# Start-up of a fused attention and MLP kernel: tile 1 on SyncE's queue in 512 B packets, ones multiplied until data come, masks of tile 2 behind MLP units, attention three units ahead

## The chip, the cores and the metric

One core of a Trainium2 chip. The metric is the device time of one execution in microseconds (us), as the median over executions; the kernel before stood at 238.68 us (238.62 to 239.02 in three executions). Profiles cover one execution and count from its first instruction, so their spans (236.7 us before) are some 2 us shorter than the times. A DMA is issued by an engine and *lands* when its data have arrived; the *tail* is the time from the last matmul's end to the end of the execution.

## The reference

Attention with 4 batches, 8 heads, 768 positions and 64 channels per head, three heads of the kind "retrieval" (causal), five "streaming" (the first four keys and a window of 64), followed by an MLP without bias on the 3072 rows of 512:

```python
stream_keep = causal & (is_sink | in_win)
mask = np.where(retr, full_mask, stream_mask)
scores = np.where(mask, scale * (q @ k.T), -1e9)
a = softmax(scores)
x = (a @ v).transpose(0, 2, 1, 3).reshape(B * S, H * D)     # 3072 x 512
h = x @ w_in                                                # 512 x 2048
return (h - np.tanh(h)) @ w_out                             # 2048 x 512
```

## The kernel before

The work is cut into 12 tiles of 256 rows. An attention unit is one tile and one pair of heads; an MLP unit is 256 columns of `h` for one tile (8 to a tile, about 2.1 us of TensorE with the output matmuls that go with it). Attention of a tile runs among the MLP units of the tile ahead of it. The Python code does not emit instructions directly. It records operations with estimated durations, simulates the engines, the two rings of DMA and their packets, and then emits the operations in the order in which the simulation started them. Each engine executes its own part of that list in order.

```python
class Plan:
    def op(self, eng, ns, fn, r=(), w=(), dma=None, prio=None, port=False, after=None, behind=None):
        ...                                   # dependencies by key; kept in self.ops
    def run(self):
        ...                                   # event simulation: who starts when
        for i in order:
            self.ops[i][2]()                  # emit
```

The loads. `paired` decides whether two neighbouring rows of q or k travel as one packet of 512 B (rows 2p and 2p+1 to partition p) or one by one in 256 B. `load` goes through SyncE in float32 and needs a cast afterwards; `load_cast` goes through GpSimd's ring and casts on the way.

```python
        def paired(nm, t):
            return nm != "v" and t == 0
        ...
        cast_qk(0, (("ACT", "ACT"), ("ACT", "DVE")), (0,))
        load_cast(1, [("rv", 0, "v", 0, 1)], "qk")        # tile 1: GpSimd's ring, 256 B
        if first:
            load_w_in(*W_IN[0], ())                       # first quarter of w_in, GpSimd's ring
            load_cast(1, (), "v")
        for n in (0, 1):
            masks(thr, "thr", range(2 * n, 2 * n + 2), added=True)
            st_T(n, "ACT", "DVE")                         # transposes of q and k on TensorE
            for f in scores(n):
                f()
        ...
        if first:
            load_w_in(*W_IN[1], ())
            load_w_in(*W_IN[2], ())
            ...
```

The plan:

```python
        AHEAD = 2.0
        for t in range(3, NTT):
            ...
            ahead = (AHEAD if t > NG else 0.0, AHEAD) if ranked(t) else (0.0, 0.0)
            SPAN[t] = (lo + cut[t % NG] - ahead[0], lo + cut[t % NG + 1] - ahead[1])
        ...
                if t == 1 and hp == HP - 1:
                    fs.append(lambda: masks(thr, "thr", range(H)))
```

The softmax here doesn't subtract the row's maximum and nothing guards it: scores larger than these inputs give would overflow.

## Time and profile before

| | before |
|---|---|
| median time | 238.68 us |
| span of the profile | 236.7 us |
| first matmul, last matmul's end | 6.0, 231.8 us |
| clock records of TensorE begin at full share | 14.95 us |
| first MLP unit | 18.93 us |
| w_in in four pieces, landed | 17.05, 23.67, 26.36, 28.98 us |
| q and k of tile 1 landed | 11.4 to 13.5 us |
| first MLP unit of tile 2, of tile 3 | 58.83, 78.75 us |

The table is read as a start-up: until 18.9 us TensorE has no MLP work. From then on the MLP is the bulk of it. The lines of the profile from which these follow are shown in the prediction.

### The profile page before, as it was taken

What the parts mean: (1) busy time and instruction counts of PE and PEld (TensorE: products, weight loads), DVE (VectorE), ACT (ScalarE), POOL (GpSimd) and SP (SyncE); (2) the same over time, 40 slices, a digit from 0 to 9 for tenths busy, and PEclk for the clock granted to TensorE, in tenths of its full rate; (3) what the DMA queues carried; (4) which work ended last, traced back from release to release, by engine and by line L of the source; (5) the groups of instructions that cost most, each with busy time, mean ns of one, the idle gap of its engine ahead of it and who ended that gap; (6) DMA issues with size and microseconds to landing.
All of it is one profiled execution on the core that took longest, in us unless ns stands there. A gap on an engine that the chain in (4) does not pass through costs nothing. (4 is left out here: it accounts for less than half of the span.)

```text
span 236.7 us, 5895 instructions
## 1 busy us (share of the span) xinstructions
PE 221.5 (94%) x2220; PEld 157.8 (67%) x2220; DVE 139.0 (59%) x343; ACT 143.6 (61%) x221; POOL 90.5 (38%) x218
## 2 busy tenths in 40 slices
PE   0889899999999999999999999999999999999991
PEld 0346687756776777777676777776776777777661
DVE  1856665864488657767666655667766546443300
ACT  3668677884588387466686649537759464444320
POOL 5999420089818068480814904606300000000000
PEclk9999999999999999999999999999999999999999
DMA  5999999999997999979989695998712101310121
GB/s 128 209 140 172 204 181 204 197 228 224 206 225 182 151 248 184 227 153 206 239 168 214 136 186 130 186 171 179 134 47 66 38 31 47 90 38 9 44 89 51
DMA packets 108130, 35.29 MB, mean 149 GB/s; under 512 B 100290, under 2 KB 104642, under 8 KB 108098
## 3 DMA queue, kind: packets, MB, share of 16 engines
q1 hardware_dynamic: 92642, 28.98, 60.5%
q0 software_dynamic: 15168, 5.77, 20.7%
q8 instruction: 18, 0.29, 0.5%
q10 hardware_dynamic: 288, 0.14, 0.2%
q14 instruction: 14, 0.11, 0.2%
HBM read 27.27 MB, written 6.29 MB: 142 GB/s over the span
## 5 line engine op out<-in xcount | busy, mean ns | idle before, releaser
L1135 PE MATMUL ph<-xT,win 128*128 128x256 f16 x768 | 101.7, 273 | 0.6 <-DMA win<-in_moe_w_in_dram 0.3
L1194 PE MATMUL po<-wout,gt 128*128 128x512 f16 (+1 forms) x400 | 98.0, 371 | 0.3 <-ACT ot L1170 0.3
L1148 ACT ACTIVATE th<-ph 128x512 f32<-128x512 f32 x96 | 57.6, 601 | 59.6 <-PE ph L1135 58.2
L1155 DVE SCALAR_TENSOR_TENSOR gt<-th,ph 128x512 f16<-128x512 f32 x96 | 65.4, 684 | 44.9 <-ACT th L1148 44.4
L1135 PEld LDWEIGHTS <-win 128*128 128x128 f16 x768 | 80.0, 114 | 13.0 <-issue 1.9
L961 ACT ACTIVATE pt<-sc 128x1024 f16<-128x1024 f32 (+1 forms) x78 | 68.5, 926 | 11.4 <-PE sc L941 10.9
L1194 PEld LDWEIGHTS <-gt 128*128 128x128 f16 x400 | 36.4, 98 | 24.6 <-issue 0.9
L680 POOL CAST t<-raw_rqk 128x256 f16 x72 | 28.5, 440 | 63.3 <-DMA raw_rqk<-in_k_dram 48.1
L1030 PEld LDWEIGHTS <-pt 128*128 128x128 f16 x552 | 25.9, 98 | 10.4 <-issue 0.9
L1030 PE MATMUL av<-v,pt 128*128 128x65 f16 x304 | 26.0, 195 | 0.1
L941 PE MATMUL sc<-qk 64*128 64x128 f16 (+1 forms) x412 | 23.8, 240 | 1.7 <-DVE qk L826 1.7
L941 PEld LDWEIGHTS <-qk 64*128 64x128 f16 x412 | 13.7, 94 | 13.5 <-issue 8.9
L675 POOL CAST v<-raw_rv 128x128 f16 x72 | 21.1, 335 | 4.2 <-DMA raw_rv<-in_v_dram 4.2
L1060 DVE TENSOR_TENSOR x16t<-av,rinv 128x128 f32 x72 | 20.8, 289 | 2.3 <-DVE rinv L1050 0.3
L1030 PE MATMUL av<-vf,pt 128*128 128x65 f16 x248 | 19.6, 193 | 0.0
L1170 ACT ACTIVATE ot<-po 128x512 f32<-128x512 f32 (+1 forms) x24 | 14.3, 596 | 8.5 <-PE po L1194 8.4
L996 DVE TENSOR_TENSOR pt<-pt,m 128x1024 f16<-128x1024 f16 x16 | 12.3, 768 | 8.0 <-ACT pt L961 8.0
L1050 DVE RECIPROCAL rinv<-av 128x4 f32<-128x4 f32 x48 | 8.6, 179 | 13.4 <-PE av L1030 13.4
L986 DVE TENSOR_TENSOR pt<-pt,mS 128x512 f16<-128x512 f16 x24 | 9.8, 449 | 6.7 <-ACT pt L961 6.7
L843 PEld LDWEIGHTS <-t 128*128 128x128 f16 x48 | 3.9, 107 | 8.9 <-ACT t L644 6.8
L523 DVE TENSOR_SCALAR m<-A,thr 128x512 f16<-128x512 f16 x16 | 7.4, 501 | 1.7 <-PE sc L928 1.2
L751 POOL TENSOR_TENSOR vf<-v,rflagr 128x260 f16<-128x260 f16 x12 | 7.5, 634 | 0.0
(95 smaller groups left out, 90.8 us busy)
## 6 DMA issues: line engine op xcount, KB each, us to landing
out_dram<-ot SPq DMA_DIRECT2D x23, 256.0 KB, 2.3
raw_rqk<-in_q_dram SPq DMA_DIRECT2D x20, 256.0 KB, 4.7
raw_rqk<-in_k_dram SPq DMA_DIRECT2D x20, 256.0 KB, 4.5
raw_rv<-in_v_dram SPq DMA_DIRECT2D x18, 256.0 KB, 4.4
win<-in_moe_w_in_dram POOLq DMA_DIRECT2D x4, 512.0 KB, 8.8
wout<-in_moe_w_out_dram POOLq DMA_DIRECT2D x4, 512.0 KB, 12.4
raw_rv<-in_v_dram SPq DMA_DIRECT2D x4, 128.0 KB, 4.7
t<-in_q_dram POOLq DMA_DIRECT2D x4, 128.0 KB, 9.5
```

The costliest lines, as they stand in the source:

```text
L675: nc.gpsimd.tensor_copy(out=v1s[b]()[:, lo : lo + NB, rank : rank + 1, 0:D], in_=raw_of("v", t)[:, :, at, :],)
L680: nc.gpsimd.tensor_copy(out=t16[t % 2][:, :, :, rank : rank + 1, :], in_=raws["rqk", t][0]()[:, :, :, at, :],)
L941: nc.tensor.matmul(out=sc()[:, hh, o : o + nb * 128].rearrange("p (i c) -> p i c", c=128), lhsT=ks.rearrange("p i c -> p (i c)")[p_, jb * ...
L961: lambda pt=pt, gi=gi, wid=wid, sc=sc: nc.scalar.activation(out=pt()[:, :, 512 * gi : 512 * gi + wid], in_=sc()[:, :, 0:wid], func=AF.Exp, ...
L996: nc.vector.tensor_mul(out=pv, in0=pv, in1=m4[:, h0 : h0 + 2, 256:512].unsqueeze(2).to_broadcast([128, 2, 2, 256]),)
L1030: nc.tensor.matmul(out=av()[:, i, hh, :], lhsT=pt()[:, hh, co : co + 128], rhs=vv, start=(jb == first_jb), stop=(jb == qb),)
L1060: nc.vector.tensor_mul(out=x16s[t]()[:, :, at, :], in0=av()[:, :, hh : hh + 1, 0:D], in1=rinv()[:, :, hh : hh + 1].unsqueeze(3).to_broadca ...
L1135: nc.tensor.matmul(out=ph()[:, j, :], lhsT=w()[:, cb, c0 + fb % 4 : c0 + 512 : 4], rhs=xTs[t]()[:, cb, :], start=(cb == 0), stop=(cb == HP ...
L1148: lambda: nc.scalar.activation(out=th()[:], in_=ph()[:], func=AF.Tanh, scale=1.0 / XS),
L1155: lambda: nc.vector.scalar_tensor_tensor(out=gts[t]()[:, u * FU : (u + 1) * FU, :], in0=th()[:], scalar=-XS, in1=ph()[:], op0=ALU.mult, op ...
L1170: nc.scalar.activation(out=ot()[:, c0:c1], in_=po()[:, c0:c1], func=AF.Copy, scale=1.0 / XS)
L1194: nc.tensor.matmul(out=po()[:, c0:c1], lhsT=gts[t]()[:, f, ts * 128 : ts * 128 + 128], rhs=w_out_t[f // 4]()[:, f % 4, c0:c1], start=(f == ...
```

## The change

The intent: shorten the start-up. TensorE multiplies ones from 1.2 us so that its clock is up when data come; tile 1's q and k go through SyncE in 512 B packets, so that GpSimd is free to issue the weights sooner; VectorE's masks of tile 2 wait until the second MLP unit is through; attention from the second batch on is planned three MLP units ahead instead of two. The fillers (more multiplications of ones) go into planned holes of TensorE up to the first transpose of x. The core of the diff:

```diff
@@ Plan.run: emission, with fillers
-    def run(self):
+    def run(self, fill=None, until=None):
...
         for i in order:
+            if self.ops[i][0] == "PE":
+                idle = self.start[i] - free
+                if self.fill and idle > 200 and i != until and self.FROM < free:
+                    self.fill(int(idle * 0.5 / 107), 256)
+                free = max(free, self.start[i] + self.ops[i][1])
+                if i == until:
+                    self.fill = None
             self.ops[i][2]()
@@ loads in pairs
-            return nm != "v" and t == 0
+            return nm != "v" and t < 2 and (first or not t)
@@ the ones
+            def run_up(n=10, c=512):
+                for _ in range(n):
+                    nc.tensor.matmul(out=wm()[:, 0:c]..., lhsT=ones[:], rhs=ones[:]..., start=True, stop=True)
+            op("PE", 2130, run_up, r=["ones"], w=[key])
@@ start
-        load_cast(1, [("rv", 0, "v", 0, 1)], "qk")
         if first:
-            load_w_in(*W_IN[0], ())
+            load(1, "qk", (0,))
+            load(1, "qk", (1,))
+            cast_qk(1, (("POOL", "POOL"), ("POOL", "POOL")))
+        cast_v(0, ("POOL", "POOL"), (0,))
+        cast_v(0, ("POOL", "POOL"), (1,))
+        if first:
+            load_w_in(*W_IN[0], raw_keys("q", 0, 1))
             load_cast(1, (), "v")
@@ the plan
-        AHEAD = 2.0
+        AHEAD = 3.0
...
-                    fs.append(lambda: masks(thr, "thr", range(H)))
+                    fs.append(lambda: masks(thr, "thr", range(H), behind=[("gt",0,1)]))
```

Cut: some estimates and one rule of the simulation (they emit nothing, but they alter the order that it plans), and the calls whose order alone moves.

More of the change, by code (lines that the diff above doesn't have):

```diff
@@ L24 @@
     PSUM = ("sc", "m", "h", "o")
+    FROM = 5800
     RESULT = {"PE": 200, "ACT": 0, "DVE": 0, "POOL": 0, "SP": 0}
@@ L39, in op @@
                 deps.add(self.writer[k])
-            if k[0] in self.PSUM:
+            if isinstance(k, tuple) and k[0] in self.PSUM:
                 deps.update(j for j in self.readers.get(k, ()) if self.ops[j][0] != eng)
@@ L57, in op @@
         return i
-    def run(self):
+    def run(self, fill=None, until=None):
+        self.fill = fill
         n = len(self.ops)
@@ L134, in run @@
             _, ns, _, _, dma, _, port, _ = self.ops[i]
+            if e == "PE" and t < 5600:
+                ns *= 2
             self.start[i] = t
@@ L140, in run @@
             for u in followers[i]:
-                ready[u] = max(ready[u], t + ns)
+                ready[u] = max(ready[u], free[e])
                 left[u] -= 1
@@ L147, in run @@
                 rings["POOL" if e == "POOL" else "SP"].append(
-                    [i, t + ns + (1200 if e == "POOL" else 300), each, packets * each / 16]
+                    [i, t + ns + (1200 if e == "POOL" else 1000 if t < 6000 else 400), each, packets * each / 16]
                 )
@@ L152, in run @@
         self.end = max(self.done)
+        free = self.FROM
         for i in order:
+            if self.ops[i][0] == "PE":
[5 more added lines that the diff above has]
+                    self.fill = None
             self.ops[i][2]()
@@ L261, in program @@
         rot = {}
+        fillers = []
         def bank(shape, dt, tag, name):
@@ L425, in program @@
             op(
-                "ACT", 400,
+                "ACT", 1150,
                 lambda: nc.scalar.dma_start(
@@ L431, in program @@
             )
-        for half in range(2):
-            load(0, "qk", (half,))
-            load(0, "v", (half,))
+        load(0, "q", (0,))
+        load(0, "k", (0,))
+        load(0, "v", (0,))
+        load(0, "q", (1,))
+        load(0, "k", (1,))
+        load(0, "v", (1,))
         if first:
             op("POOL", 204, lambda: nc.gpsimd.memset(ones[:], 1.0), w=["ones"])
+            wm, key = bank([128, 512], FP32, "o", "warm")
+            def run_up(n=10, c=512):
+                for _ in range(n):
+                    nc.tensor.matmul(
+                        out=wm()[:, 0:c].rearrange("p (a c) -> p a c", c=128), lhsT=ones[:],
+                        rhs=ones[:].unsqueeze(1).to_broadcast([128, c // 128, 128]),
+                        start=True, stop=True,
+                    )
+            op("PE", 2130, run_up, r=["ones"], w=[key])
+            fillers.append(run_up)
             op(
@@ L512, in program, with masks @@
             op("DVE", 165, make_rflag0, r=["sinks", "rflag"], w=["rflag0"])
-        def masks(threshold, key, heads, added=False):
+        def masks(threshold, key, heads, added=False, eng="DVE", behind=()):
             for h in heads:
@@ L521, in masks @@
                 op(
-                    "DVE", 350,
-                    lambda h=h, how=how: nc.vector.tensor_scalar(
+                    eng, {"DVE": 350, "POOL": 560}[eng],
+                    lambda h=h, how=how: engs[eng].tensor_scalar(
                         out=m4[:, h, :], in0=A4[:].rearrange("p a c -> p (a c)"),
@@ L526, in masks @@
                     ),
-                    r=[key, "A4", "A40", "A41", "A43"], w=[("m4", h // 2)], port=True,
+                    r=[key, "A4", "A40", "A41", "A43", *behind], w=[("m4", h // 2)], port=True,
                 )
@@ L879, in program @@
         first_S = {}
+        first_x = []
         def near(n):
@@ L1110, in mm @@
                     )
-            op("PE", 112, mm, r=[("x16", n), "ident"], w=[key])
+            first_x.append(op("PE", 112, mm, r=[("x16", n), "ident"], w=[key]))
             op(
@@ L1262, in program @@
         cast_qk(0, (("ACT", "ACT"), ("ACT", "DVE")), (0,))
-        load_cast(1, [("rv", 0, "v", 0, 1)], "qk")
         if first:
-            load_w_in(*W_IN[0], ())
+            load(1, "qk", (0,))
+            load(1, "qk", (1,))
+            cast_qk(1, (("POOL", "POOL"), ("POOL", "POOL")))
+        else:
+            load_cast(1, [("rv", 0, "v", 0, 1)], "qk")
+        cast_v(0, ("POOL", "POOL"), (0,))
+        cast_v(0, ("POOL", "POOL"), (1,))
+        if first:
+            load_w_in(*W_IN[0], raw_keys("q", 0, 1))
             load_cast(1, (), "v")
@@ L1270, in program @@
             masks(thr, "thr", range(2 * n, 2 * n + 2), added=True)
-            st_T(n, "ACT", "DVE")
+            st_T(n, *("ACT", "DVE"))
             for f in scores(n):
                 f()
-        cast_v(0, ("POOL", "POOL"), (0,))
         cast_qk(0, (("ACT", "ACT"), ("ACT", "DVE")), (1,))
@@ L1279, in program @@
             masks(thr, "thr", range(2 * n + 4, 2 * n + 6), added=True)
-            st_T(n + 2, "ACT", "DVE")
+            st_T(n + 2, *("ACT", "DVE"))
             for f in scores(n + 2):
@@ L1283, in program @@
             st_X(n, "o", "ACT")
-        cast_v(0, ("POOL", "POOL"), (1,))
         for n in (2, 3):
@@ L1401, in program @@
         with tc.manual_schedule():
-            P.run()
+            P.run(fillers[0] if fillers else None, first_x[0])
     program(True)
```

## The prediction

> **What bounds the kernel now.** I read the page first, then busy time by stretch, then the timelines of TensorE, VectorE and GpSimd for the first 30 us, then the landing time of each DMA.
>
> The page and the table by stretch:
>
> ```profile
> PE 221.5 (94%) x2220; PEld 157.8 (67%) x2220; DVE 139.0 (59%) x343; ACT 143.6 (61%) x221; POOL 90.5 (38%) x218
> ...
> 6.00:15.00 9.00, 8.12 (x56) 3.85 (x57) 6.21 (x16) 6.00 (x11) 8.77 (x12) 1.00 1.62 179
> 15.00:20.00 5.00, 4.00 (x51) 2.72 (x50) 3.23 (x12) 3.90 (x8) 5.00 (x7) 1.00 1.43 143
> 20.00:30.00 10.00, 8.78 (x116) 6.34 (x115) 7.09 (x18) 7.38 (x14) 6.53 (x8) 1.00 1.29 201
> 30.00:40.00 10.00, 9.70 (x101) 8.13 (x99) 5.86 (x12) 7.09 (x14) 1.23 (x3) 1.00 1.67 192
> 40.00:50.00 10.00, 9.34 (x123) 7.05 (x122) 8.26 (x36) 8.52 (x15) 1.74 (x5) 1.00 1.02 209
> 50.00:200.00 150.00, 149.71 (x1559) 107.11 (x1558) 95.85 (x229) 96.76 (x143) 64.18 (x172) 1.00 0.83 162
> ```
>
> TensorE (first column after the length) is the bound, but its busy time is the union of modelled latencies and hides holes. So I counted issue slots, start to start, from the dense runs of the timeline: 109 ns for a 256-column matmul, 216 for 512, 30 for the 65-column ones, 56 for 128. 768 x 109 = 83.7 us, the output matmuls 82.8, attention values 16.6, scores 15.2, the rest 7.0: **205.5 us of work that no part of this change alters**. The first matmul starts at 6.0 us and the last ends near 231.8. Of those 225.5 us, 20 are dead slots. They lie unevenly: 6.9 us between 6.0 and 18.9, about 3.4 from 18.9 to 30, 2.6 from 30 to 50, and only about 0.45 per 10 us after that, none after 200. The tail (5 us) and the first 6 us are not touched. So the change can win only in the first 50 us, and 10 of the 13 us there lie before 30.
>
> Why they are dead: first, slow matmuls.
>
> ```profile
> 12.66 0.40 PE L843 MATMUL tp3k<-ident,t 128*128 128x128 f16 x2
> 12.85 0.85 PE L928 MATMUL sc<-m,ident 128*128 128x384 f16 x2
> ...
> 18.40 0.28 PE L843 MATMUL tp5k<-ident,t 128*128 128x128 f16 x2
> ...
> 19.83 0.59 PE L928 MATMUL sc<-m,ident 128*128 128x512 f16 x2
> ```
>
> The same pair of transposes takes 0.40 us before and 0.28 after; a mask pair of 384 columns 0.85 us before, a larger one of 512 columns 0.59 after. The clock records begin at full share only 15.0 us into the span; the clock column above prints 1.00 where there is no record. Second, a chain over engines and data:
>
> ```profile
> 16.00 0.18 DVE L1050 RECIPROCAL rinv<-av 128x4 f32<-128x4 f32 x1
> 16.10 0.59 DVE L523 TENSOR_SCALAR m<-A,thr 128x512 f16<-128x512 f16 x1
> 16.61 0.40 DVE L1074 TENSOR_TENSOR x<-av,rinv 128x256 f16<-128x256 f32 x1
> ...
> 17.07 0.28 PE L1108 MATMUL xp<-ident,x 128*128 128x128 f16 x2 [0.62 <-DVE x L1074]
> ...
> 23.72 0.63 PE L1135 MATMUL ph<-xT,win 128*128 128x256 f16 x4 [0.30 <-DMA win<-in_moe_w_in_dram]
> 25.04 0.40 PE L941 MATMUL sc<-qk 64*128 64x256 f16 x6 [0.69 <-DVE qk L826]
> ```
>
> A mask of tile 2 sits on VectorE between the reciprocal and the scaling that the transpose waits for. Then the third MLP unit waits for the second piece of w_in (landed 23.67). After it the scores wait for a copy on VectorE, where two masks took 1.42 us from 23.37.
>
> **What the Trainium skill says.** "TensorE: Matmul & The Clock Gate", Part 1, has the clock at half rate until about 3.4 us of sustained matmuls, seen through a free-running window. The trace agrees on the two speeds, not on a fixed budget: scattered work from 6.0 needed until 15.0. Part 4 adds that transposes do not count as busy; so fillers that are real matmuls are the right medicine. "DMA: Bandwidth & Descriptors", Specifications, wants transfers of at least 512 B: in the trace 512 B packets of q and k run at about 750 per us, 256 B reads near 1000 (casting ones 1150), so 512 packets take 0.7 us and 1024 take 0.9. Its section "Queues, rings and completion order" has the engines go round-robin between queues by packet: where two queues run together in this trace, packets alternate about evenly. "SBUF — State Buffer", Who interferes with whom: GpSimd and a fast VectorE copy lock each other out. The masks show it: 0.34 us at best, 0.59 and 0.71 here.
>
> **The change part by part.**
>
> (a) Ones multiplied: 10 matmuls of 512 columns at half speed, 427 ns each by that page's formula, 4.3 us from about 1.2 us: over near 5.5, before the first transpose at 6.0. They delay nothing. Ten transpose pairs gain 0.12 us each, the 8 mask matmuls 0.16 each, 4 score groups 0.1, 3 value groups 0.17: 3.4 us of issue time. Not all on the path: to the first MLP unit the chain runs through one first mask group (0.6), two later ones, a transpose, three value groups: I take 1.5 us. The fillers use at most half of planned holes and should cost under 0.2 us.
>
> (b) Masks of tile 2 behind the second MLP unit: 0.34 + 0.59 us leave VectorE at 15.7 to 16.7; on the chain about 0.5. All eight now crowd between 20 and 30 us, where VectorE is 71% busy, and the 0.7 us waits for copies may stay.
>
> With (a) and (b) the first MLP unit moves from 18.93 to about 17. Alone this would then wait for w_in piece two.
>
> (c) Tile 1's q and k: today four GpSimd issues (0.88 to 1.1 us each, 3.8 us) and 4096 packets of 256 B, landing 11.4 to 13.5. GpSimd is busy from 5.2 to 24 without a hole, so the first piece of w_in is issued at 11.13 and the second at 15.81. The packet records show the DMA engines half idle from 12.5 to 14.0 and again about 18 to 19. After: 2048 packets of 512 B on the other ring, 3.0 us of DMA against 3.5, no GpSimd issue, but four GpSimd casts of 0.62 us (2.5 us, as its casts of v today). w_in piece one goes out at about 8.3, when tile 0's last q has landed. The hole of 1.4 us closes, 0.5 are saved in packets, and about half of the second hole: **w_in piece two lands some 2.3 us earlier**, near 21.4, and all later weights and tile 2 with it, because from there the engines stay full until 44 us. Cost: pair-ordered copies of tile 1's q and k take 0.44 us instead of 0.28, eight times, partly on the path: 0.2 us.
>
> (d) Attention three units ahead: a unit is about 2.1 us. It starts tiles from the second batch earlier, and squeezes tile 3. It can win the stalls at 47 (0.8 us) and 75 (0.5), if VectorE and the loads keep up; as tile 3 lands by 50 either way, I credit 0.3.
>
> Sum: (a) and (b), 2.0 us, and (c), 2.3, fill the same stretch. The shift of w_in decides what carries over: 2.3. The earlier first unit lets attention of tile 1 come before it rather than between units, which should save about 0.7 of the 3.4 dead us from 18.9 to 30. Plus 0.3 for (d), less 0.2 for copies and 0.1 for fillers: 3.0 us. 238.7 - 3.0 = **235.7 us**.
>
> **Rivals.** First, GpSimd becomes the wait: its casts for the second half of tile 1 wait for a ring that now alternates with w_in's large packets, and the issue of w_in two stands behind them. For it: 98 ns for a w_in packet against 27; against: halving GpSimd's issue work leaves slack. Then (c) gives 0.5 us: 237.3. Second, the clock isn't granted: dense work from 1.2 to 5.5 covers a whole 3.4 us window only by luck, and idle until 6 follows. Then (a) is lost; as (c) gates, the result is 236.5. Third, the startup falls as a whole: first unit at 16, w_in two by 21 and the stalls at 24 to 27 and 47 gone too: 233.5. Fourth, VectorE with eight masks in 20 to 30 loses 1 us: 236.7.
>
> **Range and chances.** 2% faster is below 233.9, which needs 4.8 of some 13 removable dead us; only the third rival gets there. 2% slower needs a fresh wait in the dense part, which has no sign for it. Range 233.8 to 237.4; faster 0.13, same 0.84, slower 0.03.
>
> **What would show it.** Right: full clock from before 9 us; transposes of tile 0 at 0.28 us; first MLP unit near 17, second w_in landing near 21.4; tile 1's q and k landing from 10 to 15; the start of the long closing run of output matmuls (223.8 now) 3 us earlier; 50 to 200 unchanged in density. Wrong: the clock turning at 12 or later; w_in two landing after 23; new waits of TensorE on copies or x at 20 to 30; new holes after 50 from attention running early.

## More of the kernel before

From tile 3 on (the second batch) the heads are sorted by kind, GpSimd casts q, k and v head by head, and SyncE issues DMA transposes of `qk` and, at the end of the tile's attention, of the attention result (`xT`), for which the first MLP unit of the tile waits:

```python
        def cast_ranked(t):                       # GpSimd
            if b not in v1s:
                ones_v(b)                         # a memset of the ones column of a new v buffer
            ...                                   # 8 heads: qk, v
            for i in range(NB):                   # SyncE, in order, behind those casts
                nc.sync.dma_start_transpose(out=qk[b % 2][...], in_=t16[t % 2][...])
        ...
        def st_X_tile(t):                         # SyncE, behind the tile's attention
            nc.sync.dma_start_transpose(out=xTs[t]()[...], in_=x16s[t]()[...])
```

## The result and the profile after

The kernel after takes **237.49 us** (median of 4, 237.35 to 237.62), the kernel before beside it 238.85 (median of 4, 238.62 to 243.15; the last is slow and does not enter the ratio). The ratio is 0.9946, interval 0.9927 to 0.9966, so it counts as the same at the 2% line. A ratio here and below is the mean time of one kernel's fast runs over that of the other's fast runs of the same rounds, so it is not quite the ratio of the medians quoted. The prediction of 235.7 was too low, and its range ended at 237.4, 0.1 us short.

The landmarks of the start-up came out as predicted or better. TensorE's timeline after (start, length, then the operation):

```profile
1.16 3.94 PE L459 MATMUL warm<-ones 128*128 128x512 f16 x10 [1.16 <-POOL ones L454]
...
10.80 0.29 PE L872 MATMUL tp3k<-ident,t 128*128 128x128 f16 x2
10.92 0.49 PE L958 MATMUL sc<-m,ident 128*128 128x384 f16 x2
...
16.01 1.50 PE L1165 MATMUL ph<-xT,win 128*128 128x256 f16 x12
...
21.66 1.06 PE L1165 MATMUL ph<-xT,win 128*128 128x256 f16 x8 [0.60 <-DMA win<-in_moe_w_in_dram]
22.65 0.39 PE L971 MATMUL sc<-qk 64*128 64x256 f16 x6
...
25.64 0.39 PE L971 MATMUL sc<-qk 64*128 64x256 f16 x6
```

The ones end at 5.1 us. The clock records show full share from 4.45 us, against 14.95 before; the transposes of `tp3k` take 0.29 us instead of 0.40, and the 384-column masks 0.49 instead of 0.85. The first MLP unit starts at 16.01, as soon as the first piece of w_in has landed (15.96). Piece two lands at 21.61 instead of 23.67. The scores at 25.64 no longer wait for a copy by VectorE. VectorE's timeline after shows why: the eight masks of tile 2 lie between 20.4 and 25.7, and the copies of q and k find their places among them. Two new waits stand in this stretch all the same: 0.62 us before `tp7k` at 24.13, for VectorE's work on an MLP unit, and 0.30 us at 29.11 for x. The prediction had named such waits as a sign of being wrong.

```profile
14.92 0.17 DVE L1080 RECIPROCAL rinv<-av 128x4 f32<-128x4 f32 x1
15.13 0.42 DVE L1104 TENSOR_TENSOR x<-av,rinv 128x256 f16<-128x256 f32 x1
...
20.45 0.92 DVE L552 TENSOR_SCALAR m<-A,thr 128x512 f16<-128x512 f16 x2
21.30 0.43 DVE L855 COPY qk<-tp6k 128x256 f16<-128x256 f16 x1
21.62 1.46 DVE L552 TENSOR_SCALAR m<-A,thr 128x512 f16<-128x512 f16 x4
```

The first part of the page and the table by stretch after (stretch and its length, then busy us of PE, PEld, DVE, ACT and POOL, the clock, DMA share and GB/s):

```profile
PE 223.4 (95%) x2234; PEld 158.4 (67%) x2234; DVE 138.9 (59%) x343; ACT 143.2 (61%) x221; POOL 90.2 (38%) x218
```

```profile
6.00:15.00 9.00, 7.47 (x90) 4.25 (x90) 6.29 (x20) 7.44 (x14) 7.53 (x10) 1.00 1.23 248
15.00:20.00 5.00, 4.70 (x55) 3.19 (x54) 2.25 (x8) 4.27 (x8) 5.00 (x8) 1.00 1.62 193
20.00:30.00 10.00, 8.48 (x98) 6.15 (x99) 7.57 (x19) 7.11 (x13) 5.01 (x7) 1.00 1.49 195
...
50.00:200.00 150.00, 149.15 (x1554) 107.07 (x1552) 95.73 (x229) 95.03 (x141) 63.06 (x167) 1.00 0.80 158
```

The last line is the first sign of the loss: after 50 us TensorE is busy 149.15 of 150 us, before it was 149.71. Busy time hides most of it. So I took every matmul of both traces, gave each its issue slot of the prediction (205.5 us in all, the same in both kernels; multiplied ones count nothing), and asked how much of that work was done at each moment. The **lead** below is what the kernel after has done more than the kernel before at the same moment, in us of TensorE. The second row is a repetition of the kernel after, profiled on another chip (run `e5_after_again` below), against the same profile of before:

| at (us) | 15 | 20 | 30 | 50 | 60 | 70 | 80 | 90 | 140 | 200 | last matmul | end |
|---|---|---|---|---|---|---|---|---|---|---|---|---|
| after | 1.25 | 2.33 | 2.07 | 2.61 | 2.71 | 2.25 | 1.76 | 1.37 | 1.49 | 1.76 | 1.70 | 0.98 |
| after, again | 1.25 | 2.33 | 2.13 | 2.82 | 2.93 | 2.36 | 1.98 | 1.59 | 1.70 | 1.76 | 1.90 | 0.96 |

At 60 us the lead is 2.7 to 2.9: the predicted sum was 3.0. Then two things go wrong. **Between 60 and 90 us 1.3 us are lost** (and some 0.4 come back later), and **0.7 to 0.9 us more are lost after the last matmul**. Neither stretch was in the prediction's sum.

### Where 60 to 90 loses

Waits of TensorE between 50 and 95 us (what waited, for what, then total, times and longest), before and then after:

```profile
PE po L1194 <- ACT ot L1170: 0.3, 1, 0.3
```

```profile
PE ph L1165 <- DMA xT<-x16t: 0.4, 1, 0.4
PE po L1224 <- ACT ot L1200: 0.3, 1, 0.3
PE av L1060 <- DVE pt L1021: 0.2, 1, 0.2
```

The first MLP unit of tile 3 waits for the transposed attention result, which it did not before (0.4 us in the profile's count, 0.52 beyond the issue slot). Tile 2's first unit had started 2.30 us earlier (56.53 against 58.83), tile 3's started only 0.82 earlier (77.93 against 78.75). The transposes were issued 1.8 us earlier and landed later. SyncE's queue shows it, before and then after:

```profile
59.91 2.61 SPq L698 DMA_TRANSPOSE qk<-t  x2
...
73.92 2.50 SPq L1088 DMA_TRANSPOSE xT<-x16t  x2
```

```profile
59.33 2.70 SPq L727 DMA_TRANSPOSE qk<-t  x2
...
72.09 2.53 SPq L1118 DMA_TRANSPOSE xT<-x16t  x2
```

The trace's landing records give 76.22 and 77.53 before, 77.24 and 77.89 after: 2.3 us from issue to landing became 5.2 for the first of the two. One profile is a thin base here: in e8, e12 and e15 below, which have the order of before on every engine, the first landed at 77.31, 77.71 and 77.14, 3.9, 4.0 and 3.4 us after its issue, and no wait came of it, since TensorE got to tile 3 at 78.3 or later. The loads ahead of the transposes in SyncE's queue land hardly earlier than before: tile 5's last k at 70.05 (69.70 before), tile 6's q at 73.58 and 74.68 (74.02 and 74.88). The `qk` transposes of tile 4, further up in the same queue, were issued only 0.6 us earlier, although TensorE was 2.3 us ahead; SyncE stood at them for a while (from 57.2 to 59.3) with all later loads behind. They wait for tile 4's casts on GpSimd. GpSimd's timeline, before and then after:

```profile
56.83 2.47 POOL L680 CAST t<-raw_rqk 128x256 f16 x7
```

```profile
54.31 0.31 POOL L814 MEMSET v<- 128x48 f16 x1 [0.97 <-PE av L1060]
54.69 1.05 POOL L789 COPY vf<-v 64x1040 f16<-64x1040 f16 x1
...
56.24 2.48 POOL L709 CAST t<-raw_rqk 128x256 f16 x7
```

The memset prepares the third buffer of v, which is the first one used again, so it waits until TensorE has read the old contents. In the plan it lies ahead of tile 4's casts now; before, it lay at 64.02 and waited for nothing. GpSimd executes its list in order and stands for 0.97 us. The memset stands ahead of the casts in e1, e3 and e4 below as well, so attention's distance, the masks or tile 1's ring did not put it there on their own; what did is not shown.

### Where the tail loses

After the last matmul the program evacuates one piece, stores it, and SyncE works through a list of 20 waits on semaphores at 0.06 to 0.10 us each (read from the trace's records; the views do not print them). The compiled program gives the DMAs of SyncE and ScalarE eight semaphores in turn, as the records of all twenty traces have it. Before, the last store had the fifth place in that list: four waits were through when it landed (234.73), and the end came 2.01 us later. Tile 1 adds four transfers on SyncE, the last store moves to the first place, and all 20 waits come after its landing (232.98): the end came 2.78 us later. Of the 0.77 us, 0.40 are in the waits (1.36 us from the landing to the list's last wait, against 0.96), and the remaining 0.37 in pauses of 0.38 to 0.49 us between closing instructions, of which after has two and before one. They might be fetches of instructions, but nothing in the trace says so: in after no packet of the two instruction queues is under way between 232.55 and 235.38, while the pauses begin at 234.37 and 235.20.

### The profile page after: what moved, and what is told of

Same layout as the page of the kernel before. It is cut to its first block, busy times and chain, and to the rows that moved or that the text cites. A ratio compares the mean times of both kernels' runs of the same rounds, so it can differ in the third digit from the quotient of the medians.

```text
span 235.8 us, 5930 instructions
## 1 busy us (share of the span) xinstructions
PE 223.4 (95%) x2234; PEld 158.4 (67%) x2234; DVE 138.9 (59%) x343; ACT 143.2 (61%) x221; POOL 90.2 (38%) x218
## 5 line engine op out<-in xcount | busy, mean ns | idle before, releaser
L1060 PEld LDWEIGHTS <-pt 128*128 128x128 f16 x552 | 25.1, 97 | 9.8 <-DVE pt L1021 0.7
L1060 PE MATMUL av<-v,pt 128*128 128x65 f16 x304 | 25.5, 193 | 0.2 <-DVE pt L1021 0.2
L704 POOL CAST v<-raw_rv 128x128 f16 x72 | 21.8, 335 | 4.0 <-DMA raw_rv<-in_v_dram 4.0
L971 PE MATMUL sc<-qk 64*128 64x128 f16 (+1 forms) x412 | 23.1, 236 | 0.0
L1016 DVE TENSOR_TENSOR pt<-pt,mS 128x512 f16<-128x512 f16 x24 | 10.4, 473 | 7.7 <-ACT pt L991 7.7
L872 PEld LDWEIGHTS <-t 128*128 128x128 f16 x48 | 3.2, 97 | 5.9 <-ACT t L673 2.4
L459 PE MATMUL warm<-ones 128*128 128x512 f16 (+1 forms) x14 | 4.7, 487 | 1.2 <-POOL ones L454 1.2
```

The lines of the kernel that those rows point to most:

```text
L704: nc.gpsimd.tensor_copy(out=v1s[b]()[:, lo : lo + NB, rank : rank + 1, 0:D], in_=raw_of("v", t)[:, :, at, :],)
L971: nc.tensor.matmul(out=sc()[:, hh, o : o + nb * 128].rearrange("p (i c) -> p i c", c=128), lhsT=ks.rearrange("p i c -> p (i c)")[p_, jb * ...
L1060: nc.tensor.matmul(out=av()[:, i, hh, :], lhsT=pt()[:, hh, co : co + 128], rhs=vv, start=(jb == first_jb), stop=(jb == qb),)
```

## The experiments

Six timed executions of each kernel (of before eleven). The chips differ in how much they scatter, so the profile's lead is given next to the time. The lead scatters as well: e15, whose order is that of before on every engine, is at 0.11 to 0.22 up to 100 us and at -0.32 from 140 on. All eighteen gave the right result.

### One part undone at a time

**e1_ahead2**: attention two units ahead again.

```diff
-        AHEAD = 3.0
+        AHEAD = 2.0
```

> The changed kernel with attention two units ahead again, nothing else. Instruction order is the same as the changed kernel's on every engine up to about 77 us. Theory G (the start-up lead of 2.7 us at 60 us is real, and SyncE's in-order ring on busy DMA engines takes 1.3 us of it back between 60 and 90 us, whatever the distance of attention): 237.2 to 237.8 us, the lead over the kernel before at 60 us 2.7 and at 80 us 1.8 as in the changed kernel. Rival D (running attention three units ahead is what costs): 236.7 us or less, lead at 90 us 2 us or more.

Measured: 238.51 us, ratio 0.996 (0.9915 to 1.0006), before between 238.4 and 243.2 on this chip. The profiled execution lost its start-up: the clock records show half share from 16.97 to 20.38 us and the lead at 60 us was 0.76, so this profile says nothing on the plan. Three things do follow. The emitted order is the same as after's until about 79 us, so (d) could not touch the stalls at 47 and 75 for which the prediction credited it. A wait for `xT` of tile 3 (0.4 us in the profile's count) is there with two units ahead as well. And the lead falls by 1.0 us between 60 and 90 here too, from 0.76 to -0.22, although it was small.

**e2_nowarm** and **e10_nowarm_again** (on another chip): no ones, no fillers.

```diff
             def run_up(n=10, c=512):
-                for _ in range(n):
+                for _ in range(0):
```

> The changed kernel with the same order of everything, but the ones matmuls and the fillers not emitted. Theory G: clock granted at 12 us or later, first MLP unit near 17.3 (16.0 in the changed kernel), the second w_in piece at 21.6 still; w_in gates, so half of the loss is made up there: 237.7 to 238.3 us. Rival W (the clock is the whole gain): 238.6 us or more. Rival N (the clock gains nothing because data gate): within 0.15 us of the changed kernel.

> Second try of the changed kernel without ones and fillers, order kept, on another chip. First MLP unit at 17.5 to 18.1 (15.9 with them), second w_in piece at 21.5 to 21.9, lead over the kernel before at 60 us 1.0 to 1.7 us instead of 2.7 to 2.9, time 0.5 to 1.2 us more than the changed kernel (ratio 0.997 to 1.000). If the clock gains nothing: ratio 0.995.

Measured: 239.11 and 238.71 us, ratios 0.9988 (0.9936 to 1.004) and 0.9987 (0.9942 to 1.0033). First MLP unit at 18.06 and 18.43, w_in two at 21.86 and 22.14, lead at 60 us 1.19 and 0.87. Without ones the change gains 0.1%, with them 0.5%: ones and fillers are worth about 0.4%, or 1 us of time, and 1.5 to 2.1 us of the lead at 60. In time alone this isn't clear of noise, since the intervals overlap with those of after. From 60 to 90 these two lose 1.3 and 1.1 us, as much as after does from a lead twice as large; each engine's order is that of after.

**e3_masksfree**: masks of tile 2 where they were.

```diff
-    masks(thr, "thr", range(H), behind=[("gt",0,1)])
+    masks(thr, "thr", range(H))
```

> The changed kernel with the masks of tile 2 free to run early again (the planner reorders from there). Theory G: VectorE's chain to the first MLP unit 0 to 0.5 us longer, 237.4 to 237.9 us. Rival M (crowding the eight masks between 20 and 30 us costs more than it saves): 237.2 us or less.

Measured: 240.69 us, ratio 1.0051 (0.9989 to 1.0114), on the chip with the widest scatter; the profile below is of its fastest execution (238.66), and what made the others slower isn't known. But the start was not worse at all: first MLP unit at 16.09, lead at 60 us 3.04. What it lost came later, in a single wait between 50 and 100 us:

```profile
PE ph L1165 <- DMA xT<-x16t: 1.8, 1, 1.8
```

So (b) gains nothing at the start; what it changes is the plan that follows, and there the same wait for tile 3's `xT` (issued at 72.26, landed 77.94) decides. SyncE's queue has one more load of k right ahead of these transposes (issued at 71.72; in after it stands behind them, at 74.67). e4 and e17, the other two with a wait of more than 1.5 us, have it ahead too (73.73 and 71.33); so has e18 (71.27), whose TensorE comes later and does not wait. No run moves this load alone.

**e4_tile1pool**: tile 1's q and k through GpSimd's ring again, with the ones and the fillers.

```diff
-            return nm != "v" and t < 2 and (first or not t)
+            return nm != "v" and t == 0
...
+        load_cast(1, [("rv", 0, "v", 0, 1)], "qk")
         if first:
-            load(1, "qk", (0,))
-            load(1, "qk", (1,))
-            cast_qk(1, (("POOL", "POOL"), ("POOL", "POOL")))
```

> The changed kernel with tile 1's q and k loaded by GpSimd's casting DMAs again, in 256 B reads, and v casts and the first w_in piece placed as before. Theory G: second w_in piece lands near 23.5 instead of 21.6, lead at 40 us under 0.8 us; 238.2 to 238.8 us. Rival W (the clock is the whole gain): within 0.3 us of the changed kernel.

The casts of tile 0's v go back to their places behind the loads with it. Measured: 240.31 us, ratio 1.006 (1.0 to 1.0119). GpSimd's timeline and then TensorE's:

```profile
10.21 0.89 POOL L675 CAST v<-raw_rv 128x512 f16<-128x512 f32 x1
12.30 0.62 POOL L675 CAST v<-raw_rv 128x512 f16<-128x512 f32 x1 [1.21 <-DMA raw_rv<-in_v_dram]
```

```profile
15.18 0.28 PE L1138 MATMUL xp<-ident,x 128*128 128x128 f16 x2 [0.75 <-DVE x L1104]
...
19.43 1.06 PE L1165 MATMUL ph<-xT,win 128*128 128x256 f16 x8
```

Piece two of w_in landed at 20.48, earlier than after's 21.61, and yet the first MLP unit came 3.4 us later, with the clock full from 5.0 us and piece one there at 16.22. Attention of tile 0 is late, not the weights: its v is cast at 10.21 (after: 7.47), behind the issues of seven DMAs, and its first transposed x follows at 15.18 (after: 11.25). The lead at 60 us was 1.63, so (c), with the earlier casts, is worth about 1.1 us there; most of the rest of the loss is a 2.0 us wait for `xT` from 78.4 on.

### Reproduction, the ring, and tile 5's loads

**e5_after_again**: the kernel after, unchanged, as the control.

> The changed kernel unaltered, as a control beside the next runs and because the first set of experiments ran on a chip whose times scatter by several us. Ratio to the kernel before 0.992 to 0.998. Tile 3's two x transposes land about 5 us after their issue near 72 to 74 us, and TensorE waits 0.5 us or more for them; the lead over the kernel before falls by 1 us or more between 60 and 90 us.

Measured: 237.59 us, ratio 0.9948 (0.9916 to 0.998). Its lead is the second row of the table above; both losses are there again.

**e6_actring**: a few of the bulk loads on ScalarE's queue. The theory (R in the expectations): tile 3's transposes land late because they stand behind loads in SyncE's ring.

```diff
-                            lambda ...: nc.sync.dma_start(
+                            lambda ..., by=(nc.scalar if first and (nm, t) == ("q", 6) else nc.sync): by.dma_start(
```

> The changed kernel with the two loads of tile 6's q issued by ScalarE on its own ring, at their old place in time; all else in the same order. Theory R (tile 3's x transposes lose their time behind loads in SyncE's first-in first-out ring): transposes land 2.5 to 3.5 us after issue, no wait of TensorE for them at tile 3, 0.4 to 0.8 us faster than the control. Rival B (the DMA engines as a whole are the limit, whatever the ring): landing still near 5 us, time within 0.2 us of the control. Rival D (attention's distance costs): same as rival B.

Measured: 237.07 us, ratio 0.9921 (0.9894 to 0.9947). The transposes still landed at 77.04 and 77.59 (issued at 71.41 and 72.67), TensorE still waited (0.43 us beyond the issue slot, control 0.53), and its last matmul ended at 229.82, as in the control (229.91). The ring theory falls, and that the time is the 0.5 us lower that it had forecast is chance. What this run gains over the control lies in the tail alone: 5.09 us from the last matmul to the end, against 5.87. The last store has the same first place among the semaphores in both; what is shorter is 0.47 us of pauses behind the list, 0.26 before the landing and 0.06 in the list.

**e7_t5early**: tile 5's loads allowed one tile earlier.

```diff
-   after=gated if first and t == 1 else first_S[t * HP + hp],
+   after=gated if first and t == 1 else first_S[t * HP + hp - (HP if t == 3 else 0)],
```

> The changed kernel with tile 5's loads bound to tile 2's scores instead of tile 3's, so that q and k of tile 5 stand ahead of tile 4's transposes in SyncE's order and fill the stretch near 59 us in which the DMA engines stand idle. Theory R: x of tile 3 lands within 3.5 us of issue, 0.3 to 1.0 us faster than the control; tile 4's q and k may come up to 1 us later. Rival B: within 0.2 us of the control or slower.

Measured: 238.79 us, ratio 1.0007 (0.9965 to 1.0049). The wait for `xT` is gone (72.11 to 76.26) and the lead at 80 us is 2.41 instead of the control's 1.98; but the plan behind it differs, and the lead at 140 is 0.39. So the late landing does depend on when the loads of tile 5 go out. As a remedy it fails.

**e8_before_warm** and **e12_before_fill**: the kernel before with ten multiplications of ones, and with the fillers as well.

```diff
-            op("POOL", 204, lambda: nc.gpsimd.memset(ones[:], 1.0), w=["ones"])
+            def ones_and_run_up():
+                nc.gpsimd.memset(ones[:], 1.0)
+                for _ in range(10):
+                    nc.tensor.matmul(out=wm()..., lhsT=ones[:], rhs=ones[:]..., start=True, stop=True)
+            op("POOL", 204, ones_and_run_up, w=["ones"])
```

> The kernel before, same order of everything, with only the ten ones matmuls added ahead. Theory G (w_in gates): clock granted by 8 us, first MLP unit 0.7 to 1.5 us earlier than 18.9, second w_in piece where it was (23.7), time 0 to 0.5 us under the kernel before. Rival W (the clock is the whole gain): 1.0 us or more under it.

> The kernel before, same order, with the ones matmuls and the fillers as well. Beside the run with the ones alone, whose clock fell back to half for 3.4 us near 12 us in all six executions (mean granted clock 0.979 to 0.987): with fillers the clock stays, mean 0.99 or more; lead at 60 us 0.5 to 1.0 us; ratio 0.996 to 0.999. If fillers do not hold the clock, as in the run with the ones alone.

Measured: 238.67 us, ratio 0.9983 (0.9957 to 1.0009), and 239.19 us, ratio 0.9998 (0.9945 to 1.005). With ones alone the records show full clock from 5.19 and half again from 12.02 to 15.43; with fillers it is full from 5.46 on without a break. Even so the lead at 60 us is 0.22 only (0.55 with ones alone, whose piece two of w_in landed at 22.51, in the same order of issue). TensorE's timeline with fillers:

```profile
17.69 1.06 PE L1162 MATMUL ph<-xT,win 128*128 128x256 f16 x8
...
23.58 0.63 PE L1162 MATMUL ph<-xT,win 128*128 128x256 f16 x4 [0.82 <-DMA win<-in_moe_w_in_dram]
```

The first unit gains 1.2 us and gives it back to piece two of w_in, which lands at 23.54. In the old order the clock alone gains nothing that is clear of noise, 0.2 to 0.6 us of lead; in the new order it is worth its 1 us. How much of that new order is (c) is not separated: e4, without (c), has a lead of 1.63.

### The tail

**e9_tail7**: seven DMAs of one element behind tile 1's loads, so that the semaphores of the last transfers stand seven places on.

```diff
             load(1, "qk", (1,))
+            def more():
+                for j in range(7):
+                    nc.sync.dma_start(out=extra[:, j : j + 1], in_=ones[0:1, 0:1])
+            op("SP", 50, more, r=["ones"], after=len(P.ops) - 1)
```

> The changed kernel with seven one-element transfers added on SyncE after tile 1's loads, where SyncE has nothing to do. The eight semaphores of SyncE's and ScalarE's transfers go round, so the last store's moves from first to last in the list that SyncE waits through at the end. Theory T (0.8 us of the gain was lost between the last matmul and the end, by where the last store's semaphore stands[...]): seven waits of 0.08 us pass before the last landing, last landing to end 2.2 us or less instead of 2.78, 0.4 to 0.9 us faster than the changed kernel (ratio to the kernel before 0.991 to 0.993). Rival: the tail is set by the landing alone, no change.

Measured: 236.80 us, ratio 0.9904 (0.9864 to 0.9944). Seven waits of the list now pass ahead of the landing, and the last matmul's end (230.55) is followed by 4.64 us, against 5.65 after. Of the 1.08 us between landing and end that this run saves, 0.60 are in the list and 0.47 in pauses behind it. The part in the list follows the place of the last store in nineteen of the twenty traces: 1.30 to 1.36 us from landing to the list's last wait at place one, 0.96 at place five (e4 too, where the four transfers of tile 1 are gone), 0.76 at place eight. That the order of semaphores sets this part is shown. The pauses move without it: e6 has place one and 0.47 us less of them.

**e15_before_tail3**: the same on the kernel before, with three DMAs (three places from the fifth).

```diff
+                for j in range(3):
+                    nc.sync.dma_start(out=extra[:, j : j + 1], in_=ones[0:1, 0:1])
+            op("SP", 50, more, r=["ones", *raw_keys("v", 0, 1)])
```

> The kernel before with three one-element transfers added on SyncE, which takes its last store's semaphore from fifth to last of eight: last landing to end 1.7 to 1.8 us instead of 2.0[...]; 0.1 to 0.4 us faster, ratio 0.998 to 1.000.

Measured: 238.91 us, ratio 1.0017 (0.9976 to 1.0058): no gain. Seven waits did pass early, but a pause of 0.41 us now fell inside the list, and landing to end was 2.18 us (before 2.01). This is the exception to the list above (1.16 us). The expectation had as its condition that the pauses fall as before; they did not. The waits are understood; the place of the pauses is not.

### Tile 4's casts

**e11_hoist**: SyncE issues tile 5's four q and k loads ahead of tile 4's two `qk` transposes, instead of standing at them. 

```diff
+        if self.ahead:
+            order = self.hoist(order)        # tile 5's q, k loads before tile 4's transposes
```

> The changed kernel with only SyncE's order altered: tile 5's four loads of q and k stand ahead of tile 4's two transposes; every other engine keeps its order. Theory I (the DMA engines idle near 59 us because SyncE stands at transposes that wait for GpSimd's casts, and the work left undone delays tile 3's x): tile 3's x lands at 76.3 or before, TensorE does not wait for it, lead at 80 us 2.3 us or more instead of 2.0, 0.3 to 0.8 us faster than the changed kernel. Rival: tile 4's q and k, 2 us later, hold TensorE instead, and nothing is gained.

Measured: 238.00 us, ratio 0.9957 (0.9917 to 0.9997). Tile 3's `xT` lands in time (72.44 to 76.23). The wait has only moved: the `qk` transposes of tile 4 land at 66.29 and 67.49, and TensorE waits for them, as the rival in the expectation has it.

```profile
PE sc L987 <- DMA qk<-t: 0.9, 1, 0.9
```

**e13_late_memset**: the memset emitted behind tile 4's casts. It is the shortest remedy under the theory (P in the expectations) that GpSimd's wait in front of the casts is the root.

```diff
         self.end = max(self.done)
+        if self.late is not None:                 # the memset of the third v buffer
+            order.remove(self.late)
+            at = max(n for n, i in enumerate(order) if i in self.casts)   # tile 4's casts
+            order.insert(at + 1, self.late)
```

> The changed kernel with one GpSimd instruction moved: the memset of the third v buffer stands after tile 4's casts instead of before them, where it waited 1 us for TensorE. All other orders are kept. Theory P (this wait holds back tile 4's casts, so SyncE's transposes and behind them tile 5's loads, while the DMA engines idle): tile 4's transposes issued near 58.4 instead of 59.2, tile 3's x lands near 76.2 instead of 77.1, TensorE does not wait for it, 0.4 to 0.9 us faster than the changed kernel (ratio to the kernel before 0.991 to 0.993). Rival Q (DMA throughput alone limits this stage): landing within 0.3 us of 77.1, time within 0.2 us, ratio 0.994 to 0.996.

Measured: **236.70 us** (236.40 to 237.16), ratio 0.991 (0.9887 to 0.9933). GpSimd's timeline and SyncE's queue:

```profile
54.88 2.46 POOL L715 CAST t<-raw_rqk 128x256 f16 x7
...
60.80 0.32 POOL L824 MEMSET v<- 128x48 f16 x1
```

```profile
57.96 2.61 SPq L735 DMA_TRANSPOSE qk<-t  x2
...
71.23 2.53 SPq L1128 DMA_TRANSPOSE xT<-x16t  x2
```

The casts start 1.36 us earlier than after, the transposes go out 1.37 us earlier, and TensorE's hole at 63 us is gone. Tile 6's q lands at 72.73 and 73.83, 0.85 us earlier than after. The wait for `xT` shrinks to 0.24 us (landing 76.40). The lead is 2.82 at 60, 2.52 at 80, 2.17 at 90: 0.65 lost where after lost 1.34. The order of all other engines is that of after, and the tail is as after (2.77 us from landing to end), so the gain is TensorE's. The root of about half of the loss is thus shown, by the lead; the times agree (0.991 against 0.9946 and 0.9948), but were taken on different chips, and the intervals touch. e14, e16 and e18, with the same move, have no wait for `xT` either. Rival Q is refuted as it was put (the landing moved by 0.65 to 0.84 us), but from issue to landing it still took 5.2 us. The other half stays: TensorE still waits a little for `xT`, and the plan from 80 to 90 is not the one of before. It does not lie in longer holes: those of 0.12 us or more between 55 and 95 us sum to 1.69 us before, 2.56 after and 1.63 here.

### Both remedies

**e14_late_tail7** joins e13 and e9; **e16_late_tail7_ahead2** is the same with `AHEAD = 2.0`.

> The moved memset and the seven one-element transfers together: if both terms are real and independent, the sum, 1.0 to 1.7 us faster than the changed kernel, ratio 0.987 to 0.990. If P is wrong: ratio 0.990 to 0.992, as with the seven transfers alone.

> As the run with both, with attention two units ahead. From the one pair of traces so far, three ahead was worth 0.3 us after 80 us: 0.2 to 0.5 us slower than the run with both. Rival D: 0.3 us or more faster.

Measured: 236.51 us (235.21 to 237.78), ratio 0.9899 (0.9861 to 0.9938), and **236.13 us** (235.78 to 236.45), ratio 0.9891 (0.9867 to 0.9915), the fastest median (the intervals of e9, e13 and e14 overlap with it). The profile of e16 has a lead of 2.24 at 90, 2.06 at 220, the last matmul's end at 229.72 and 4.56 us after it. Its first units wait for no `xT`. The profiled execution of e14 again had the clock fall back (16.84 to 20.25 us).

**e17_late_tail7b** and **e18_late_tail7b_ahead2**: the seven DMAs moved behind the first MLP unit, so that they can't stand in the way of w_in; attention three and two units ahead.

```diff
-            op("SP", 50, more, r=["ones"], after=len(P.ops) - 1)
+            plan.setdefault(3, []).append(lambda: op("SP", 50, more, r=[("gt", 0, 0)]))
```

> The moved memset and seven one-element transfers as before, but the seven read the first MLP unit's result, so they cannot start before about 18 us. In the three runs with the seven at 9.5 us the first w_in piece landed at 16.9 to 17.3, in most runs without them at 15.7 to 16.0. If the seven transfers delayed it: landing at 15.7 to 16.1, 0.3 to 0.8 us faster than with the seven early, ratio 0.985 to 0.989. If not: 0.989 to 0.991.

> The same with attention two units ahead, the second side-by-side pair for the distance of attention. If three ahead is worth 0.3 us: 0.2 to 0.5 us slower than the run beside it. If it is worth nothing: within 0.2 us.

Measured: 238.35 us, ratio 0.997 (0.9937 to 1.0003), and 237.02 us, ratio 0.9915 (0.989 to 0.994). The later place is no better. First pieces of w_in landed at 15.80 and 17.04 with the same start, so the tiny DMAs are not what decides that. In e17 a full start-up (lead 3.04 at 60) is spent on two waits between 76 and 98 us, and the lead is 0.13 at 100. The moved memset is thus not enough by itself; SyncE's list differs from e13's in the load of k named under e3:

```profile
PE ph L1176 <- DMA xT<-x16t: 1.6, 1, 1.6
PE sc L982 <- DMA qk<-t: 0.9, 1, 0.9
```

e18 has neither wait, although its profiled execution too had the clock fall back, and its lead is 1.2 from 100 on. In both pairs two units ahead did no worse than three, in this one it was 1.3 us faster.

## Why the prediction was wrong

The prediction's first claim, that only the first 50 us can win, was right, and its sum for them came close, in part by luck. The **step that failed** is what it took for granted outside that stretch: "50 to 200 unchanged in density", and a tail that is "not touched".

- **Start-up, the sum**: predicted 3.0 us, measured 2.7 and 2.9 at 60 us. Here luck helped: the 0.7 us that were to come between 18.9 and 30 did not (the lead falls from 2.33 at 20 to 2.07 at 30, with the new waits at 24.13 and 29.11), and some 0.8 came between 40 and 50 instead, where the stall at 47 is gone; the prediction had put that stall under (d), and it is gone with two units ahead as well (e1). The predicted landmarks: clock full before 9 us (4.45), transposes at 0.28 us (0.29), first MLP unit near 17 (16.01), w_in two near 21.4 (21.61), the first w_in issue at about 8.3 (8.04); tile 1's q and k between 10 and 15 (11.2 to 16.7, a little later). The last of them missed: the closing run of output matmuls starts at 222.14, 1.7 us earlier than the 223.84 of before and not 3. Two sums of the prediction are slightly off, without effect: its work adds up to 205.3 us, and from 6.0 to 231.8 it is 225.8.
- **(a)**: right that the clock is granted, and that in the old order other things gate. There ones and fillers give 0.22 us of lead (e12); in the new order 1.5 to 2.1 (e2, e10). That transposes do not count for the clock, which the prediction takes from the skill, no run here tests. The second rival put the loss of (a) at 0.8 us of time; measured about 1.
- **(b)**: predicted 0.5 us on the chain; measured nothing at the start (e3: 3.04 us of lead without it). That the masks' 0.34 to 0.71 us come from a lock between GpSimd and VectorE is argued in the prediction; no run tests it.
- **(c)**: right in effect, with a correction. In e4 piece two of w_in lands early and the first unit late. So (c), with the earlier casts of v, gains also by bringing attention of tile 0 sooner (its v is no longer behind the issues), not by w_in alone. A packet rate was misread: where 512 B packets of q and k run alone for 0.7 us, the records of both kernels have 500 to 620 of them per us, not 750. At these rates 2048 packets take 3.3 to 4.1 us, no less than the 3.5 us that the prediction gives for the casts, and the 0.5 us that it saves in packets are not there.
- **(d)**: credited 0.3 us; it cannot touch the stalls named, since the order is the same up to 79 us, and the runs in pairs show no gain from it.
- **"50 to 200 unchanged in density"**: failed, 1.3 us by 90, of which about 0.4 return. The order of GpSimd's list had changed: the memset of a buffer in use now stood ahead of tile 4's casts. It is the order that costs, not the earlier TensorE: with the order of after, e2, e9 and e10 start from leads of 0.87 to 2.06 and lose 1.1 to 1.3 us from 60 to 90; with the order of before, e8, e12 and e15 gain or lose 0.12 at most. SyncE stood behind the casts, the loads behind SyncE, and tile 3's transposes among the loads. The prediction looked for "new holes after 50 from attention running early"; the holes came, but from the order of one engine's list. e13 undoes that order and gets about half back.
- **The tail**: failed, 0.7 to 0.9 us in the profiles. Four more transfers on SyncE shift the turn of the semaphores, and the last store is waited for first. That is 0.40 us, shown by e9 and e4, which shift it again. The other 0.37 us in the profile of after are pauses, and their cause stays open.

With the remedies for both, and attention two units ahead (e16), the time is 236.1 us, close to the 235.7 predicted and well inside the range. What stays open: why piece one of w_in lands at about 15.9 in some executions and about 17.0 in others with the same start, what fixes the places of the pauses in the tail, and the other half of the loss from 60 to 90. Also, e14 and e17, each timed on its own chip, differ by 0.7% in their ratios for the place of seven tiny DMAs: differences of this size come from the plan as a whole, and I did not trace this one to its root.

## What to carry to other kernels

A gain at the start is not a gain at the end until each engine's in-order list has been checked behind it: ask which instruction in those lists waits for a buffer that the faster engine frees no earlier, and what stands behind it. An engine list that is planned by simulation changes everywhere when its start changes, so compare the order of both kernels' lists, not only the part that was edited. Where DMAs are added, look at the end of the program as well: which semaphore the last store has got there.

## What the Trainium skill lacked or had wrong

- "TensorE: Matmul & The Clock Gate", Part 1 ("HAM oscillation"), warns of gaps of more than about 3.4 us. In three profiles (e1, e14, e18) the clock fell to half for 3.4 us with no gap of that length: TensorE waited 1.1 to 1.4 us for w_in at most, with transposes and small matmuls in the rest. (The page's next section tells of a kernel in which short idles between groups of matmuls did the same, without saying how short.) The records change at steps of 3.41 us (full for 10.2 us, then half for 3.4), which agrees with that page's free-running window. In all three a window closed at 16.6 to 17.0 us and the first MLP matmul came after it; in e9 and e16 piece one of w_in was as late (17.25, 16.90), the windows, counted in steps of 3.41 us from the start of the full record, closed at 15.8 and 14.7 and next after 18, and the clock held.
- The same page's budget of 3.4 us of sustained work: ten dense matmuls of ones from 1.16 us brought full clock at 3.9 to 7.0 us, and without fillers it was lost again at 12.0 (e8). How dense a window must be isn't on the page; the scattered work of the kernel before needed until 14.95.
- "DMA: Bandwidth & Descriptors" says that a DMA's wait for a semaphore is done by the issuing sequencer, but doesn't draw the consequence that all its later transfers are held back, however idle the DMA engines are. Here SyncE stood from 57.2 to 59.3 us at tile 4's transposes; moving what they wait for (e13) brought them out 1.37 us sooner.
- No page has the list of waits at the end of a program: 20 waits of 0.06 to 0.10 us on SyncE, with the last store's place in the list set by the number of DMAs before it (1.30 to 1.36 us from landing to the list's last wait when first, 0.76 when eighth, in all traces but e15), and pauses of 0.38 to 0.50 us whose places vary (2.78 us from landing to end in most traces with place one, 2.24 in e6).
